# One x transpose moved to ScalarE's DMA queue, and weight loads issued ahead of the x pieces, in the opening of a gated attention-mix kernel

## Chip, cores and metric

The kernel runs on one core of a Trainium2 chip. The metric is device time in microseconds (us). The first execution ever of the kernel before took 999.06 us. It is in the 475.19 us that was known when the prediction was made (without it, 475.07). "The profile" is one recorded execution; its span is about 1.7 us shorter than the device time of the same execution. A *landing* is the moment at which the last of a load's 16 DMA engines has reported its part, as the recorded semaphore updates of the trace have it.

## The reference

Two attention blocks share the input x (2048 x 1024, bf16) and are mixed by a gate computed from x:

```python
g = sigmoid((x * gate_w).sum(-1, keepdims=True))
a = linear_attention(x, A_wqkv, A_wo)          # phi(q), phi(k), 32 heads of 32
b = dilated_sliding_attention(x, B_wqkv, B_wo) # 8 keys, 2 apart
return g * a + (1 - g) * b
```

Only the first product matters here: block A's keys, x @ wqkv[:, 1024:2048], which is the first real work of the kernel.

## The kernel before

The matmuls of this kernel take x with the contraction dimension on the partitions, so x is transposed while it is loaded (`dma_start_transpose`). For the first four row tiles (512 rows) the load is cut along the contraction into four *quarters* k. Each quarter has one x piece (512 rows x 256 columns, 256 KB) and two weight loads (half 0 and half 1 of the key columns, 256 KB each). Quarter 0's x piece comes in two transposes of 256 rows.

```python
load_wk(nc.scalar, 0, 0)                 # quarter 0, half 0: ScalarE's queue
with tc.manual_schedule(engines={SP}):   # everything else: SyncE's queue, in this order
    load_xT(0, 0, 2)                     # quarter 0, rows 0..255
    load_xT(0, 2, 4)                     # quarter 0, rows 256..511
    load_wk(nc.sync, 0, 1)
    for k in range(1, 4):
        load_xT(k, 0, 4)
        load_wk(nc.sync, k, 0)
        load_wk(nc.sync, k, 1)
    for t in range(4, NB):               # the other row tiles, whole rows
        nc.sync.dma_start_transpose(out=xT[:, :, t * P:(t + 1) * P], in_=rows(x, t * P, (t + 1) * P))
    # ... cut: further loads ...
```

TensorE first runs 34 junk matmuls on a tile of ones. Then it takes the quarters in turn, 16 matmuls each, and after them the other row tiles:

```python
warm_up(34)
first = [bank_k(i) for i in range(8)]
for k in range(4):
    for half in range(2):
        for t in range(4):
            for kt in (2 * k, 2 * k + 1):
                project(first[4 * half + t], t, kt, half)
            # ... cut: at k == 3, phi of the finished bank ...
```

A quarter can start when its x piece and its half-0 weights have landed.

## Time and profile before

| | before |
|---|---|
| median, the 3 runs known when the prediction was made (999.06 is one of them) | 475.19 us |
| TensorE busy, of a span of 473.4 us | 466.0 us |
| TensorE starts real matmuls | 4.74 us |
| quarter 1 starts | 10.33 us |

The page of the kernel before, its busy times and its chain of work that ended last:

```profile
PE 466.0 (98%) x5731; PEld 244.6 (52%) x5762; DVE 277.7 (59%) x602; ACT 169.0 (36%) x272; POOL 15.3 (3%) x30
...
PE 97%; DMA 1%; SPq 1%; issue 0%; ACT 0%
```

TensorE is on the chain nearly throughout, so a change to the loads can matter only where TensorE waits for one. The timeline of TensorE, first 24 us of the kernel before (start, duration, engine, line, operation, count, and in brackets the idle time ahead of it with what ended it):

```profile
1.11 3.81 PE L174 MATMUL warm<-onesb 128*128 128x128 bf16 x34 [1.11 <-DVE onesb L165]
4.74 4.11 PE L168 MATMUL pk_ps<-WkA,xT 128*128 128x512 bf16 x15
10.33 13.97 PE L168 MATMUL pk_ps<-WkA,xT 128*128 128x512 bf16 x63 [1.48 <-DMA WkA<-in_A_wqkv_dram]
```

(One of quarter 0's 16 matmul records is missing.) The only idle stretch of these 24 us after the start is the 1.48 us ahead of quarter 1, ended by a WkA load. The chain of the first 40 us says where that load came from (start, duration, what; a DMA line runs from the issue to the landing):

```profile
0.80 1.30 SPq L94
...
2.15 1.25 SPq L94
...
3.44 0.58 SPq L98
...
4.07 1.24 SPq L94
...
5.36 4.93 DMA WkA<-in_A_wqkv_dram
...
10.33 10.73 PE pk_ps L168 x49
```

SPq is SyncE's queue at work issuing: L94 is a transpose, L98 a weight load. The weights of quarter 1 had to wait behind three transposes of about 1.25 us each and a weight load. Issued at 5.36, they landed at 10.29.

### The profile page before, as it was taken

How to read it: one execution, taken by the hardware profiler on the slowest of the kernel's cores; microseconds unless marked ns; L12 is line 12 of the kernel's file. 1: busy time of each engine (PE TensorE's matmuls, PEld its weight loads, DVE VectorE, ACT ScalarE, POOL GpSimd, SP SyncE). 2: the span in 40 equal slices, each digit the busy share in tenths (PEclk: the TensorE clock that was granted, in tenths of full speed). 3: DMA queues.
4: the chain of work that ended last, by engine and by line, in shares of the span. 5: the costliest groups of instructions: out<-in, count | busy, mean ns of one | idle time of the engine just before them, and what ended most of it. 6: DMA issues, size and time to landing. Idle time of an engine off the chain costs nothing.

```text
span 473.4 us, 13138 instructions
## 1 busy us (share of the span) xinstructions
PE 466.0 (98%) x5731; PEld 244.6 (52%) x5762; DVE 277.7 (59%) x602; ACT 169.0 (36%) x272; POOL 15.3 (3%) x30
## 2 busy tenths in 40 slices
PE   7999999999999999999999999999999999999997
PEld 5444444444444444445666666666664444444444
DVE  0496689991329999999567676767560049800000
ACT  1343321102443333333555555555551134221122
POOL 2300000500000000000000000000000000000000
PEclk9999999999999999999999999999999999999999
DMA  8999980000644233627327455442663923221111
GB/s 168 231 225 381 349 269 0 0 1 0 204 133 111 96 137 126 161 96 241 106 57 101 81 85 94 102 91 51 91 167 73 200 90 78 68 55 45 35 34 45
DMA packets 98780, 55.40 MB, mean 117 GB/s; under 512 B 70178, under 2 KB 90658, under 8 KB 98722
## 3 DMA queue, kind: packets, MB, share of 16 engines
q1 hardware_dynamic: 93554, 50.10, 42.3%
q10 hardware_dynamic: 5168, 4.46, 2.9%
q8 instruction: 45, 0.74, 0.7%
q14 instruction: 13, 0.11, 0.1%
HBM read 26.10 MB, written 15.86 MB: 89 GB/s over the span
## 4 chain that ended last, share of the span: by engine, by line
PE 97%; DMA 1%; SPq 1%; issue 0%; ACT 0%
PE q_ps L387 26%; PE d_ps L584 12%; PE p_ps L294 12%; PE g_ps L219 12%; PE e_ps L584 11%; PE pk_ps L168 11%; PE p_ps L330 9%; PE po L466 2%; PE s2b L444 2%; DMA WkA<-in_A_wqkv_dram 1%; SPq L94 1%; PE kv_ps L239 0%; PE w_ps L282 0%; SPq L98 0%; ACT osb L589 0%
## 5 line engine op out<-in xcount | busy, mean ns | idle before, releaser
L387 PE MATMUL q_ps<-xT,WqB 64*64 64x512 bf16 x1024 | 68.3, 377 | 0.0
L387 PE MATMUL q_ps<-xT,WkB 64*64 64x512 bf16 x1024 | 67.9, 377 | 0.0
L153 DVE TENSOR_SCALAR e<-e 128x512 f32<-128x512 f32 x64 | 27.1, 423 | 64.5 <-ACT e L152 64.5
L294 PE MATMUL p_ps<-WvB,xT 128*128 128x512 bf16 x250 | 57.3, 379 | 0.5 <-issue 0.3
L168 PE MATMUL pk_ps<-WkA,xT 128*128 128x512 bf16 x251 | 55.9, 383 | 1.7 <-DMA WkA<-in_A_wqkv_dram 1.5
L219 PE MATMUL g_ps<-pk,xrow 128*128 128x512 bf16 x251 | 55.2, 379 | 0.3
L449 ACT ACTIVATE PT<-s2b 128x928 bf16<-128x928 f32 (+4 forms) x40 | 34.1, 854 | 45.6 <-PE s2b L444 45.6
L451 DVE TENSOR_TENSOR PT<-PT,mask 128x928 bf16<-128x928 bf16 (+4 forms) x40 | 23.6, 590 | 37.8 <-ACT PT L449 37.8
L330 PE MATMUL p_ps<-WqA,xT 128*128 128x512 bf16 x187 | 43.1, 379 | 0.3
L168 PEld LDWEIGHTS <-xT 128*128 128x128 bf16 x256 | 25.1, 99 | 32.0 <-issue 2.5
L584 PEld LDWEIGHTS <-pqT 128*128 128x128 bf16 x272 | 26.0, 98 | 29.8 <-issue 0.4
L584 PEld LDWEIGHTS <-OBT 128*128 128x128 bf16 x272 | 26.0, 98 | 29.4
L219 PEld LDWEIGHTS <-xrow 128*128 128x128 bf16 x256 | 25.1, 98 | 30.2
L294 PEld LDWEIGHTS <-xT 128*128 128x128 bf16 x256 | 24.6, 98 | 30.0 <-issue 0.9
L387 PEld LDWEIGHTS <-WkB 64*64 64x64 bf16 x1024 | 31.8, 107 | 15.4 <-issue 0.4
L387 PEld LDWEIGHTS <-WqB 64*64 64x64 bf16 x1024 | 31.5, 106 | 15.5 <-issue 0.9
L152 ACT ACTIVATE e<-pk_ps 128x512 f32<-128x512 f32 x32 | 18.9, 597 | 42.0 <-PE pk_ps L168 36.6
L299 ACT CAST tmp<-p_ps 128x512 bf16<-128x512 f32 x32 | 18.7, 589 | 37.6 <-PE p_ps L294 31.2
L584 PE MATMUL d_ps<-WoA,pqT 128*128 128x512 bf16 (+1 forms) x133 | 30.7, 370 | 0.2
L584 PE MATMUL d_ps<-WoB,OBT 128*128 128x512 bf16 (+1 forms) x134 | 30.7, 370 | 0.1
L330 PEld LDWEIGHTS <-xT 128*128 128x128 bf16 x192 | 18.8, 98 | 22.7
L584 PE MATMUL e_ps<-WoB,OBT 128*128 128x512 bf16 (+2 forms) x133 | 29.7, 363 | 0.2
(62 smaller groups left out, 484.1 us busy)
## 6 DMA issues: line engine op xcount, KB each, us to landing
vd<-tmp SPq DMA_DIRECT2D x16, 264.0 KB
xrow<-in_A_x_dram SPq DMA_DIRECT2D x4, 1024.0 KB
out_dram<-osb ACTq DMA_DIRECT2D x31, 128.0 KB
pqd<-tmp SPq DMA_DIRECT2D x12, 256.0 KB
WvA<-in_A_wqkv_dram SPq DMA_DIRECT2D x2, 1024.0 KB
WoA<-in_A_wo_dram SPq DMA_DIRECT2D x2, 1024.0 KB
WvB<-in_B_wqkv_dram SPq DMA_DIRECT2D x2, 1024.0 KB
WqA<-in_A_wqkv_dram SPq DMA_DIRECT2D x2, 1024.0 KB
```

The costliest lines, as they stand in the source:

```text
L152: nc.scalar.activation(out=e[:], in_=pj[:], func=ACT.Exp)
L153: nc.vector.tensor_scalar(out=e[:], in0=e[:], scalar1=1.0, scalar2=1e-6, op0=ALU.min, op1=ALU.add)
L168: nc.tensor.matmul(pj[:], lhsT=xT[:, kt, t * P:(t + 1) * P], rhs=WkA[half][:, kt, :], start=(kt == 0), stop=(kt == KT - 1))
L219: nc.tensor.matmul(pj[:], lhsT=xrow[:, t, kt * P:(kt + 1) * P], rhs=pk[:, t, half * 512:(half + 1) * 512], start=(t == 0), stop=(t == NB - 1))
L294: nc.tensor.matmul(st["pj"][:], lhsT=xT[:, kt, t * P:(t + 1) * P], rhs=WvB[half][:, kt, :], start=(kt == 0), stop=(kt == KT - 1))
L299: nc.scalar.copy(out=v[:, half * 16:(half + 1) * 16, 0:Dh], in_=st["pj"][:].rearrange("p (h e) -> p h e", h=16))
L330: nc.tensor.matmul(st["pj"][:], lhsT=xT[:, kt, t * P:(t + 1) * P], rhs=WqA[half][:, kt, :], start=(kt == 0), stop=(kt == KT - 1))
L387: nc.tensor.matmul(banks[o][64 * j:64 * j + 64, :], lhsT=lhsT(r, kt, j), rhs=rhs(r, kt), start=first and kt == 0, stop=kt == KT - 1, skip_ ...
L444: nc.tensor.matmul(s2b[64 * par:64 * par + 64, pair, :, o:o + w], lhsT=kts[c][r, par, k0:k0 + 64], rhs=qz[r, :, par, q0 % 512:q0 % 512 + w ...
L449: nc.scalar.activation(out=pt[:, :, 0:W_], in_=s2b[:].rearrange("p a b s -> p (a b) s")[:, :, 0:W_], func=ACT.Exp, scale=SCALE)
L451: nc.vector.tensor_tensor(out=pt[:, :, 0:W_], in0=pt[:, :, 0:W_], in1=mask[:, None, base:base + W_].broadcast_to([P, 4, W_]), op=ALU.mult)
L584: nc.tensor.matmul(st["ps"][:, 0:n], lhsT=lhsT, rhs=W[c0 // 512][:, c, c0 % 512:c0 % 512 + n], start=(side == 0 and c == 0), stop=(side == ...
```

## The change

The intent is to get those weights issued sooner: one of the three transposes goes to ScalarE's queue, which issues nothing after its one weight load (0.82 to 1.27) in the opening, and each quarter's half-0 weights go ahead of its x piece.

```diff
-    def load_xT(k, t0, t1):
-        nc.sync.dma_start_transpose(out=xT[:, 2 * k:2 * k + 2, t0 * P:t1 * P],
-                                    in_=rows(x, t0 * P, t1 * P)[:, 2 * k * P:(2 * k + 2) * P])
+    def load_xT(eng, k, t0, t1):
+        eng.dma_start_transpose(out=xT[:, 2 * k:2 * k + 2, t0 * P:t1 * P],
+                                in_=rows(x, t0 * P, t1 * P)[:, 2 * k * P:(2 * k + 2) * P])
 ...
     load_wk(nc.scalar, 0, 0)
+    load_xT(nc.scalar, 0, 2, 4)
     with tc.manual_schedule(engines={SP}):
-        load_xT(0, 0, 2)
-        load_xT(0, 2, 4)
+        load_xT(nc.sync, 0, 0, 2)
         load_wk(nc.sync, 0, 1)
         for k in range(1, 4):
-            load_xT(k, 0, 4)
             load_wk(nc.sync, k, 0)
+            load_xT(nc.sync, k, 0, 4)
             load_wk(nc.sync, k, 1)
```

## The prediction

> **What bounds the kernel now.** TensorE: the page's busy table gives PE 466.0 of 473.4 us, and the chain that ended last is 97% PE. Outside the opening TensorE hardly idles (the waits view names one real wait: 1.5 us for a WkA load). So only the opening can move, and any change of the moment at which TensorE becomes continuously busy passes to the end one for one.
>
> The opening, from timeline, chain and landing records: junk matmuls run to 4.74 us; quarter 0 (16 matmuls) runs 4.74 to 8.85, the first four at a pitch of 0.43 us, the rest at 0.216; then idle until 10.33, because WkA quarter 1 half 0 (issued by SyncE at 5.36) landed at 10.29. From there TensorE is continuous. Landings: x piece 0 first half 4.70, second half 5.30; WkA quarter 0 3.73 and 6.98; x piece 1 7.99. A transpose costs its queue 1.24 to 1.30 us to issue, a weight load 0.5 to 0.6.
>
> **Intent.** Taking one transpose (1.25 us) from SyncE and issuing quarter 1's weights before its x piece puts that load at about 2.7 us instead of 5.36. At most it recovers the 1.48 us idle.
>
> **What the change adds.** The built program shows what the diff does not: transposes on two queues are chained. ScalarE's transpose waits for the completion of SyncE's first one, and SyncE's next transpose (x piece 1) waits for the completion of ScalarE's. The Trainium skill, page "DMA: Bandwidth & Descriptors", section "Silent corruption: two transposing streams in flight at once", says that the later stream's first transpose must wait for the earlier stream's full completion; the trace of before, with one stream, cannot show it. So three transposes that overlapped (issues 0.80, 2.15, 4.07) now run one after another, each with issue, transfer and completion exposed.
>
> Estimate from before's durations:
> - First half lands about 4.6 (before 4.70).
> - ScalarE issues then; issue to landing was 3.15 us for the 256-token piece (2.15 to 5.30): second half lands about 7.8 (before 5.30).
> - SyncE issues x piece 1 then; issue to landing was 3.9 us (4.07 to 7.99), perhaps a little less on a quiet queue: lands about 11.6 (before 7.99).
>
> TensorE: first four matmuls 4.74 to 6.45, idle to 7.8, twelve more (12 x 0.216) to 10.4, idle to about 11.7 to 12, then continuous. Quarter 1 starts about 1.3 to 1.8 us later than 10.33. If the first gap keeps the matmuls at 0.43 us, quarter 0 ends near 13 and the loss is 2.7 us. Later quarters: before, x and weights of a quarter arrived about every 2.5 us while TensorE takes 3.45 us, so no new stall after quarter 1 is expected; xrow and later loads shift but have slack.
>
> **Predicted time: 476.8 us (before 475.2), 80% range 475.4 to 478.8.** Chance of faster by over 2%: 0.005; within 2%: 0.985; slower by over 2%: 0.01.
>
> **What would show the steps.** Right: ScalarE's transpose issue appears at about 4.7, not 1.3; SyncE's queue is empty from about 3.3 to 7.8; a first TensorE gap before x's second half, a second one ended by x piece 1 (an xT transpose, no longer WkA); WkA quarter 1 half 0 lands before 7; from about 12 everything is before's timeline shifted by a constant. Wrong: transposes overlap, or quarter 1 starts before 10.3.
>
> **What would make it wrong.** Lone transposes land much faster than 3.15 and 3.9 us (then a tie or small gain); before's late WkA landing (engines spread from 8.60 to 10.29) is a stall that another order avoids or meets again at x piece 1; ScalarE issues transposes more slowly than SyncE; the gap delays the 0.216 us pace; a later quarter stalls because SyncE's queue restarts near 8 us.

## The result, and the profile after

The changed kernel's median is 475.87 us (475.70 to 476.76, 6 runs), the kernel before's 474.51 us in the five runs counted with it (474.73 if the 999.06 is counted too). The ratio is 1.003, 95% interval 1.0017 to 1.0044: slower, by an amount far inside 2%. A ratio here is the mean time of one kernel's fast runs over that of the other's of the same rounds, so it is not quite the ratio of the medians.

The page after, the same two lines:

```profile
PE 466.4 (98%) x5731; PEld 244.3 (52%) x5762; DVE 277.7 (59%) x602; ACT 169.1 (36%) x272; POOL 15.4 (3%) x30
...
PE 97%; DMA 2%; issue 0%; ACT 0%
```

The work is unchanged; the chain's DMA share has grown, and SyncE's issuing has left the chain. The timeline of TensorE after:

```profile
4.72 1.91 PE L168 MATMUL pk_ps<-WkA,xT 128*128 128x512 bf16 x4
7.82 2.55 PE L168 MATMUL pk_ps<-WkA,xT 128*128 128x512 bf16 x11 [1.19 <-DMA xT<-in_A_x_dram]
11.02 13.28 PE L168 MATMUL pk_ps<-WkA,xT 128*128 128x512 bf16 x59 [0.65 <-DMA xT<-in_A_x_dram]
```

Where there was one gap there are now two, and both end with an x transpose, not with weights. The chain after:

```profile
0.80 3.46 DMA xT<-in_A_x_dram
...
4.28 3.49 DMA xT<-in_A_x_dram
...
7.79 3.18 DMA xT<-in_A_x_dram
...
11.02 10.91 PE pk_ps L168 x49
```

Three transposes run strictly one after another: each is issued 0.02 us after the one before it has landed. The timelines of ScalarE's and then SyncE's queue after agree:

```profile
4.28 1.29 ACTq L94 DMA_TRANSPOSE xT<-in_A_x_dram  x1
```

```profile
0.80 1.29 SPq L94 DMA_TRANSPOSE xT<-in_A_x_dram  x1
2.15 1.07 SPq L98 DMA_DIRECT2D WkA<-in_A_wqkv_dram  x2
7.79 1.25 SPq L94 DMA_TRANSPOSE xT<-in_A_x_dram  x1
```

ScalarE has issued its weight load by 1.26, but issues its transpose only at 4.28. SyncE stands still from 3.22 to 7.79. The weights that were late before are early now: in the landing records, quarter 1's half 0 lands at 6.71. But quarter 1 starts 0.69 us later than before (11.02 against 10.33), because its x piece now lands at 10.97 instead of 7.99. By the first matmul of the next stage the shift is 0.85 us (62.98 against 62.13), and at the end of the span it is 0.84 (474.2 against 473.4). From that matmul to the end both profiles take 411.2 us: everything after the opening is only carried along.

Call the wait of a transpose on one queue for the landing of a transpose on the other a *handover*. The changed kernel has two of them in the opening, ScalarE's behind SyncE's first and SyncE's next behind ScalarE's.

### The profile page after: what moved, and what is told of

Its sections match the earlier page's. It is cut to its first block, busy times and chain, and to the rows that moved or that the text cites. A ratio compares the mean times of both kernels' runs of the same rounds, so it can differ in the third digit from the quotient of the medians.

```text
span 474.2 us, 13138 instructions
## 1 busy us (share of the span) xinstructions
PE 466.4 (98%) x5731; PEld 244.3 (52%) x5762; DVE 277.7 (59%) x602; ACT 169.1 (36%) x272; POOL 15.4 (3%) x30
## 4 chain that ended last, share of the span: by engine, by line
PE 97%; DMA 2%; issue 0%; ACT 0%
PE q_ps L387 26%; PE d_ps L584 12%; PE p_ps L294 12%; PE g_ps L219 12%; PE e_ps L584 11%; PE pk_ps L168 11%; PE p_ps L330 9%; DMA xT<-in_A_x_dram 2%; PE po L466 2%; PE s2b L444 2%; PE kv_ps L239 0%; PE w_ps L282 0%; ACT osb L589 0%
```

## The experiments

The theory: the handovers cost the time; the new order of the loads, alone, costs nothing and gains a little. Rivals: the order itself delays x; ScalarE's queue is slow at transposes; two queues in use hinder each other at the DMA engines; the clock of TensorE. All kernels gave correct results. Each was timed in 5 rounds beside the kernel before, on the same chip for e1 to e4; e5 to e8; the three repeats; e9.

| run | handovers before quarter 1 | quarter 1 starts, us | median, us | before, us | ratio (95% interval) |
|---|---|---|---|---|---|
| changed kernel | 2 | 11.02 | 475.87 | 474.51 | 1.0030 (1.0017 to 1.0044) |
| e1_reorder | 0 | 9.09 | 473.91 | 474.51 | 0.9987 (0.9975 to 0.9999) |
| e2_move | 2 | 11.65 | 476.49 | 474.51 | 1.0050 (1.0036 to 1.0063) |
| e3_weights_act | 0 | 9.61 | 474.22 | 474.51 | 0.9994 (0.9982 to 1.0006) |
| e4_x_act | 0 | 12.26 | 477.21 | 474.51 | 1.0061 (1.0049 to 1.0073) |
| e5_mirror | 0 | 9.51 | 474.24 | 474.94 | 0.9989 (0.9976 to 1.0001) |
| e6_one_handover | 1 | 9.77 | 474.69 | 474.94 | 0.9996 (0.9983 to 1.0009) |
| e7_four_handovers | 4 | 16.54 | 481.42 | 474.94 | 1.0134 (1.0117 to 1.0151) |
| e8_four_sync | 0 | 10.43 | 475.20 | 474.94 | 1.0012 (0.9999 to 1.0024) |
| before_again | 0 | 9.46 | 474.30 | 474.79 | 0.9995 (0.9983 to 1.0008) |
| after_again | 2 | 12.03 | 476.71 | 474.79 | 1.0037 (1.0025 to 1.0050) |
| e1_again | 0 | 9.23 | 473.99 | 474.79 | 0.9987 (0.9973 to 1.0001) |
| e9_filled_gap | 2 | 10.55 | 476.46 | 474.87 | 1.0033 (1.0018 to 1.0049) |

### The two halves of the change, each alone: e1 and e2

e1_reorder takes the order of the change without the move:

```diff
     load_wk(nc.scalar, 0, 0)
-    load_xT(nc.scalar, 0, 2, 4)
     with tc.manual_schedule(engines={SP}):
         load_xT(nc.sync, 0, 0, 2)
+        load_xT(nc.sync, 0, 2, 4)
```

> The second half of the change alone: each quarter's first weights ahead of its x piece, all transposes on SyncE, so no transpose waits for another queue. Theory (handovers between queues cost the time, the order does not): x piece 1 is issued at about 4.6 us and lands at 8.3 to 8.9, WkA quarter 1 half 0 before it; TensorE's quarter 1 starts at 8.9 to 9.3 instead of 10.33 (before) and 11.02 (after); time about 1.0 to 1.5 us below before. Rival (weights ahead of x delay the x pieces): quarter 1 starts at 10.3 or later, waits for xT, time at or above before.

Measured: 473.91 us, 0.6 below before (1.0 to 1.5 had been expected; a likely reason is before's own late load, below: in its repeat quarter 1 starts at 9.46, only 0.37 after e1's 9.09). The timeline of TensorE shows no gap left, one unbroken group from the end of the warm-up to past quarter 3:

```profile
4.83 19.53 PE L168 MATMUL pk_ps<-WkA,xT 128*128 128x512 bf16 x84
```

So the order does not delay x enough to matter: x piece 1 lands at 8.97, and quarter 0 lasts until then.

e2_move takes the move without the order:

```diff
         for k in range(1, 4):
-            load_wk(nc.sync, k, 0)
             load_xT(nc.sync, k, 0, 4)
+            load_wk(nc.sync, k, 0)
             load_wk(nc.sync, k, 1)
```

> The first half of the change alone: the second transpose on ScalarE's queue, SyncE's order as before. Theory: ScalarE's transpose is issued when the first one has landed (about 4.3) and lands at 7.8, x piece 1 lands at about 11.0 as in the changed kernel, and WkA quarter 1, now issued behind it at about 9.1, lands at 11.5 to 12.2; quarter 1 starts then; time 0.5 to 1.2 us above the changed kernel, 1.6 to 2.3 above before. Rival (the new order of the loads is what cost the time): at or below before.

Measured: 476.49 us, 2.0 above before and 0.6 above the changed kernel. (One of its six runs, 478.34 with a granted clock of 0.996, lies 1.8 above the others.) The chain of e2_move:

```profile
0.80 3.29 DMA xT<-in_A_x_dram
...
4.12 2.73 DMA xT<-in_A_x_dram
...
6.87 1.25 SPq L94
...
8.16 3.45 DMA WkA<-in_A_wqkv_dram
```

The two handovers stand at the head of the chain, and the weights then wait behind the delayed transpose. The four versions fit a sum: order alone 0.9987, move alone 1.0050, both 1.0030 and (repeat) 1.0037. The product of the first two is 1.0037. The move costs about 2 us, the order gives back about 0.6. That 0.6 is a net gain. In the changed kernel, where quarter 1's weights are issued ahead, ScalarE's transpose took 3.49 us from issue to landing; in e2, with one weight load fewer issued before it, 2.73.

### Relieving SyncE with ordinary loads: e3

Against e1; quarters 2 and 3 keep the order of the kernel before:

```diff
     load_wk(nc.scalar, 0, 0)
+    load_wk(nc.scalar, 0, 1)
+    load_wk(nc.scalar, 1, 0)
     with tc.manual_schedule(engines={SP}):
         load_xT(nc.sync, 0, 0, 2)
         load_xT(nc.sync, 0, 2, 4)
-        load_wk(nc.sync, 0, 1)
 ...   (cut: the rest of the loop)
```

> SyncE relieved by moving ordinary loads instead: quarter 0's second and quarter 1's first weight load on ScalarE's queue, all transposes on SyncE, no handover. Theory: transposes are issued at 0.8, 2.1 and 3.4, x piece 1 lands at 7.5 to 8.5, both weight loads before it; quarter 1 starts at about 8.9, time 1.2 to 1.5 us below before. Rival (two queues in use at once slow each other at the DMA engines): x's halves land later than 4.70 and 5.30 by a microsecond or more and the gain is under 0.5 us.

Measured: 474.22 us, 0.3 below before and inside the noise. Here the rival's numbers came true. The halves of x landed at 5.78 and 6.97 instead of 4.70 and 5.30, and TensorE's first matmul waited until 5.82. The transposes were issued on time (0.80, 2.16, 3.44), so the delay is in the transfer. The Trainium skill, page "DMA: Bandwidth & Descriptors", section "Issuing engines are not separate DMA queues", says that DMAs from all issuing engines run on the same 16 DMA engines and that a second issuer saves only sequencer time. This run agrees: two more weight loads issued early on the other queue (three in all) cost the first transposes 1.1 and 1.7 us.

### Is ScalarE's queue bad at transposes? e4 and e5

e4_x_act puts all five transposes of the x pieces on ScalarE and the other weights on SyncE (against the changed kernel):

```diff
     load_wk(nc.scalar, 0, 0)
+    load_xT(nc.scalar, 0, 0, 2)
     load_xT(nc.scalar, 0, 2, 4)
+    for k in range(1, 4):
+        load_xT(nc.scalar, k, 0, 4)
     with tc.manual_schedule(engines={SP}):
-        load_xT(nc.sync, 0, 0, 2)
         load_wk(nc.sync, 0, 1)
         for k in range(1, 4):
             load_wk(nc.sync, k, 0)
-            load_xT(nc.sync, k, 0, 4)
             load_wk(nc.sync, k, 1)
```

> All five transposes of the four x pieces on ScalarE's queue, all weights but the first on SyncE; only one handover, at SyncE's transpose of row tile 4, needed by TensorE only near 19 us. Theory: ScalarE issues them without waits at 1.25 us each from 1.3; x lands at about 4.7, 5.9 and 8.5; quarter 1 starts at about 8.9 to 9.3, no gap later; time 0.8 to 1.5 us below before. Rival (ScalarE's queue is slow at transposes, or issues them late): x's second half lands at 7 or later again, time at or above the changed kernel.

Measured: 477.21 us, the opposite of what the theory had said. The chain of e4_x_act:

```profile
1.34 6.06 DMA xT<-in_A_x_dram
...
7.45 4.75 PE pk_ps L169 x15
```

The first transpose was issued at 1.34 without any handover, but took until 7.40 to land. By 2.82 SyncE had issued four weight loads and ScalarE one, 1.25 MB, which share the DMA engines with it. Its last two transposes took 2.67 and 3.08 us to issue. The late landing is not the whole loss: TensorE's first seven matmuls then came about 0.43 us apart, and quarter 1 began at 12.26 although its x piece had landed at 11.02. This run cannot tell crowding from a slow ScalarE queue, so e5 was built: the opening of e1 with the two queues exchanged, same order, no crowd ahead of the transposes.

```diff
-    load_wk(nc.scalar, 0, 0)
-    with tc.manual_schedule(engines={SP}):
-        load_xT(nc.sync, 0, 0, 2)
+    load_wk(nc.sync, 0, 0)
+    with tc.manual_schedule(engines={mybir.EngineType.Activation}):
+        load_xT(nc.scalar, 0, 0, 2)
 ...   (all of e1's opening on nc.scalar; an issue-order edge keeps row tile 4 behind it)
```

> The opening of e1_reorder with the two queues exchanged: ScalarE issues all five transposes and seven weight loads in the same order, SyncE the first weight load and then the row tiles. One handover, at row tile 4, which TensorE needs only near 19.8 us. This takes the crowding of e4_x_act away. Theory (ScalarE's queue is as good for transposes as SyncE's): halves of x land at 4.7 to 5.3 and 5.3 to 6.0, quarter 1 starts at 9.0 to 9.8, time within 0.7 us of e1_reorder (473.2 to 474.6). Rival (transposes from ScalarE are slow in themselves): the issues take over 2 us each or the halves land past 6.5, and the time is at or above the changed kernel, 475.9.

Measured: 474.24 us, ratio 0.9989 against e1's 0.9987. ScalarE's first two transposes took 1.28 and 1.29 us to issue and landed at 4.43 and 5.60. ScalarE's queue is as good for transposes as SyncE's. That leaves the crowd as the likely cause of e4's late landing, which no run isolated further. The one handover that e5 has, at row tile 4, cost TensorE nothing: SyncE issued that tile at 15.14, it landed at 18.98, and TensorE reached it at 19.88. (What TensorE did wait for in e5, 1.02 us, was quarter 0's half-1 weights, which landed at 7.66.)

### The number of handovers: e6, e7 and e8

e6_one_handover has both halves of piece 0 on ScalarE, followed there by the next two weight loads, and x piece 1 as SyncE's first transpose. (An issue-order edge between the transposes keeps the scheduler from exchanging them; it is not a wait.)

```diff
     load_wk(nc.scalar, 0, 0)
+    load_xT(nc.scalar, 0, 0, 2)
     load_xT(nc.scalar, 0, 2, 4)
+    load_wk(nc.scalar, 0, 1)
+    load_wk(nc.scalar, 1, 0)
     with tc.manual_schedule(engines={SP}):
-        load_xT(nc.sync, 0, 0, 2)
-        load_wk(nc.sync, 0, 1)
-        load_wk(nc.sync, 1, 0)
         load_xT(nc.sync, 1, 0, 4)
```

> The changed kernel with one handover instead of two: both halves of x piece 0 on ScalarE, followed there by the next two weight loads; x piece 1 is SyncE's first transpose and waits for the second half. Theory (each handover exposes one whole transpose, about 2.7 to 3.5 us): halves land at 4.7 to 5.3 and 5.7 to 6.3, x piece 1 is issued at once then and lands 3.2 us later at 9.0 to 9.6, quarter 1 starts there; time 1.0 to 1.8 us below the changed kernel (474.1 to 474.9), about level with before. Rival (it is ScalarE's use that costs, not the number of handovers): at 475.5 or above.

Measured: 474.69 us, 1.2 below the changed kernel and level with before. The chain of e6:

```profile
2.63 3.09 DMA xT<-in_A_x_dram
...
5.80 3.92 DMA xT<-in_A_x_dram
...
9.77 20.30 PE pk_ps L178 x93
```

One handover is left (SyncE issues at 5.80, when ScalarE's second has landed at 5.72). x piece 1 took 3.92 us here, with two weight loads underway beside it, so it landed at 9.72, 0.1 us later than expected.

e7_four_handovers splits piece 0 into four transposes of 128 rows on alternating queues; e8_four_sync is its control, all on SyncE:

```diff
         load_xT(nc.sync, 0, 0, 1)
         load_wk(nc.sync, 0, 1)
         load_wk(nc.sync, 1, 0)
-        load_xT(nc.sync, 0, 1, 2)      # e8
+        load_xT(nc.scalar, 0, 1, 2)    # e7
         load_xT(nc.sync, 0, 2, 3)
-        load_xT(nc.sync, 0, 3, 4)      # e8
+        load_xT(nc.scalar, 0, 3, 4)    # e7
         load_xT(nc.sync, 1, 0, 4)
```

> Four handovers: x piece 0 in four transposes of 128 rows, alternating SyncE, ScalarE, SyncE, ScalarE, then x piece 1 on SyncE. Theory: first lands at 3.6 to 4.1, then 2.3 to 2.9 us for each further one (9.2 or so for the third, 11 to 12.5 for the fourth), x piece 1 another 3.2 later; quarter 1 starts at 14.3 to 15.8; time 3.3 to 4.8 us above the changed kernel (479 to 481). Rival (the order of the loads or DMA bandwidth sets the opening): under 477.

> Control for e7_four_handovers: the same four small transposes and the same order of loads, all on SyncE, no handover. Theory: nothing of e7's loss is due to smaller transposes; the fourth lands at 6.5 to 7.3, x piece 1 at 9 to 9.8, quarter 1 starts at 9.0 to 9.9; time 473.8 to 474.8, 4.5 to 6.5 us below e7. Rival (small transposes are slow): over 476.

Measured: e7 481.42 us, e8 475.20 us, 6.2 us apart. The timeline of TensorE in e7:

```profile
4.58 0.59 PE L179 MATMUL pk_ps<-WkA,xT 128*128 128x512 bf16 x2
7.29 0.60 PE L179 MATMUL pk_ps<-WkA,xT 128*128 128x512 bf16 x2 [2.12 <-DMA xT<-in_A_x_dram]
9.89 1.03 PE L179 MATMUL pk_ps<-WkA,xT 128*128 128x512 bf16 x2 [2.00 <-DMA xT<-in_A_x_dram]
12.30 12.07 PE L179 MATMUL pk_ps<-WkA,xT 128*128 128x512 bf16 x42 [1.37 <-DMA xT<-in_A_x_dram]
```

Every handover shows as a gap. From issue to landing they took 3.35, 2.58, 2.38 and 2.97 us. Both kernels missed their expectations slightly, and both misses teach something.

e7 lost more than the handovers: x piece 1 had landed at 15.24, but quarter 1 started at 16.54, because the last ten matmuls of quarter 0 ran at a pitch of 0.43 us. The stretches of e7 (bounds, length, busy time of PE and the other engines, granted clock PEclk, DMA share, GB/s) show the clock:

```profile
8.00:12.00 4.00, 1.03 (x2) 0.13 (x2) 0.00 (x0) 0.00 (x0) 2.00 (x5) 0.50 0.15 33
12.00:18.00 6.00, 5.70 (x14) 2.11 (x15) 0.00 (x0) 0.00 (x0) 4.82 (x16) 0.50 0.74 161
```

e8 was 0.4 us above its range. Its profile points to the issuing: a transpose cost its queue about the same to issue whatever its size. The timeline of SyncE in e8 shows four of them issued in a row:

```profile
3.25 5.11 SPq L96 DMA_TRANSPOSE xT<-in_A_x_dram  x4
```

That group is the last three transposes of 128 rows and then x piece 1 (1.19, 1.25, 1.25 and 1.30 us, the last with four times the rows). So the fourth small transpose was issued only at 5.77 and landed at 8.21 (expected 6.5 to 7.3); the ten matmuls that were left of quarter 0 ran on from there to 10.43, where quarter 1 starts. x piece 1, issued at 7.06 instead of e1's 4.58, landed at 10.14, just before.

### Repeats, and the clock: before_again, after_again, e1_again, e9

The three kernels were run again, unchanged, together on one chip.

> The kernel before, unchanged, as a copy: the noise floor of the comparison, and a second profile. The ratio to before should hold 1.000 within 0.0015. Open: whether the late landing of WkA quarter 1 half 0 at 10.29 us (some DMA engines at 8.6, the last at 10.29) is usual. If it is a property of this order of loads, quarter 1 starts at 10.0 to 10.6 again; if it was a chance stall, quarter 1 starts at 8.9 to 9.6 and the profiled span is about a microsecond shorter.

> The changed kernel, unchanged, as a copy, on the same chip as e1_again: a second profile of the two handovers. ScalarE's transpose lands at 7.4 to 8.0 and x piece 1 at 10.7 to 11.3 again; time 0.8 to 1.5 us above before and 1.4 to 2.4 us above e1_again.

> e1_reorder again, on the same chip as the two kernels it is compared with: 0.3 to 1.2 us below before, no gap in TensorE's opening after 4.9 us, quarter 1 starting at 8.9 to 9.5. If its gain over before was chance, the ratio to before holds 1.000 within its interval and lies above 0.9995.

before_again gave 0.9995: the floor of the comparison. Its profile, however, differs from before's. Quarter 1's weights landed at 9.42 there and not at 10.29, and quarter 1 started at 9.46:

```profile
9.46 14.84 PE L168 MATMUL pk_ps<-WkA,xT 128*128 128x512 bf16 x67 [1.06 <-DMA WkA<-in_A_wqkv_dram]
```

In both records some of the DMA engines finish that load over a microsecond ahead of the last (8.60 to 10.29 in before, 8.27 to 9.42 in before_again). Similar stragglers appear at other loads in other runs, such as quarter 0's half 1 in e1_again (6.08 to 7.37), where TensorE waited 0.49 us for it though no gap had been expected. What makes them straggle was not found. So the idle that the change could have recovered is 1.0 to 1.5 us, not a fixed 1.48.

e1_again gave 0.9987, as e1 did. This version is the fastest in both series, though by only 0.13% against before. The interval excludes 1 in one of the two series and just includes it in the other; the profiles, in which quarter 1 starts 9.09 and 9.23 against 10.33 and 9.46, say why.

after_again gave 476.71 us, again slower than both, by 1.9 and 2.7 us: more than the 0.8 to 1.5 and 1.4 to 2.4 expected. The handovers are those of the first profile (issues at 0.80, 4.32 and 7.80, landings at 7.79 and 11.23). But in the profiled execution the clock also fell. The stretches of after_again:

```profile
5.00:8.00 3.00, 0.71 (x4) 0.18 (x3) 0.00 (x0) 0.00 (x0) 0.00 (x0) 0.95 0.59 159
8.00:12.00 4.00, 3.98 (x11) 1.45 (x11) 0.00 (x0) 0.00 (x0) 2.25 (x6) 0.61 0.65 131
```

and its timeline of TensorE:

```profile
4.52 1.03 PE L168 MATMUL pk_ps<-WkA,xT 128*128 128x512 bf16 x4
7.83 16.45 PE L168 MATMUL pk_ps<-WkA,xT 128*128 128x512 bf16 x66 [2.29 <-DMA xT<-in_A_x_dram]
```

Here TensorE was at full pace from 4.52, so its first four matmuls were done early and the gap was 2.29 us instead of 1.19. After it, eight matmuls came at 0.43 us apart, quarter 0 ended at 12.0, and x piece 1, landed at 11.23, had to wait 0.8 us for it. Quarter 1 started at 12.03 instead of 11.02. The Trainium skill, page "TensorE: Matmul & The Clock Gate", section "What's actually happening", says that TensorE's clock gate watches a free-running window of activity, so that the moment of the switch differs from run to run. The profiles agree in the effect: the first real matmuls had a pitch of 0.43 us in the first profiles of before and after, 0.22 in both kernels' repeats.

Does that clock explain the upper ones of the changed kernel's runs (476.7 to 476.9, four of five with a granted clock of 0.996, against 475.6 to 476.0 at 1.0)? In the profiled execution the clock was 0.50 from 7.7 to 11.1; by an estimate from that, half clock for 3.4 of 475 us makes a mean of 0.996, so one such stretch would account for the clock of these runs. e7's runs point the same way, the lower clock with the longer time: two at 0.989 took 482.01 and 482.41, two at 0.993 took 480.67 and 480.82. e9 fills the first gap with junk matmuls:

```diff
                     for t in range(4):
+                        if k == 0 and half == 0 and t == 2:
+                            for i in range(24):
+                                nc.tensor.matmul(first[4][:, 0:P], lhsT=onesb[:], rhs=onesb[:], start=True, stop=True)
                         for kt in (2 * k, 2 * k + 1):
```

> The changed kernel with 24 junk 128-column matmuls on TensorE between row tiles 1 and 2 of quarter 0 (into a bank whose first real matmul clears it), so that TensorE is hardly idle while ScalarE's transpose lands; the queues and both handovers are as in the changed kernel. Theory (the changed kernel's upper runs, 476.7 to 476.9 with a granted clock of 0.996, are those in which the 2.3 us gap drops TensorE's clock): no run shows 0.996, all lie at 475.4 to 476.2, quarter 0's later matmuls follow at 0.216 us, and quarter 1 still starts at 10.8 to 11.4 because x piece 1 lands no earlier. Rival (the upper runs come from the DMA side, a later landing of x piece 1): runs still spread to 476.7 and above.

Measured: 476.46 us (476.09 to 476.80). The granted clock was 0.999 or more in all six runs, quarter 0's later matmuls followed at 0.216 us, and quarter 1 started at 10.55 (expected 10.8 to 11.4), so filling the gap kept the clock. The time did not come down, though: five of the six runs lie above the expected 475.4 to 476.2. The timeline of TensorE in e9 shows a wait that no other profile had there:

```profile
16.47 7.71 PE L168 MATMUL pk_ps<-WkA,xT 128*128 128x512 bf16 x34 [0.33 <-DMA WkA<-in_A_wqkv_dram]
```

Quarter 2's half-1 weights, issued at 11.03, landed at 16.43, and TensorE was ready for them at about 15.99 (15.77 for the start of the matmul before, plus 0.216). Quarter 2 itself had started 0.2 us late, at 14.24, when its x piece landed at 14.20. Even so, by the first matmul of the next stage e9 is only 0.10 us behind the changed kernel's first profile (63.09 against 62.98). The other half microsecond of its longer span (474.9 against 474.2) lies outside the opening: the waits of e9 have 0.5 us at `po` (L469), in block B, that no other profile has. From the first matmul of the next stage to the end, twelve of the fourteen profiles take 411.2 to 411.3 us, e9's 411.8 and e5's 412.0; e5's profiled run, 475.05, was also about 0.8 above its other four. What makes this late difference was not looked into.

So the low clock is shown as a cost of the gap in the profiles of after_again and e7, but it is not the only cause of the changed kernel's upper runs: one run of after_again at clock 1.0 took 476.71 too. How much belongs to the clock, to stragglers and to the late difference stays open.

What was not tried: transposes on two queues without the wait. The price of the wait is therefore read from the number of handovers, not from taking it away.

## Why the prediction was right or wrong

- **The bound and the place: right.** Only the opening moved. The shift at the next stage (0.85 us) equals that of the span (0.84 us).
- **The hidden waits: right.** The built program chains the transposes, and the chain after shows them issued 0.02 us after the one before has landed. The Trainium skill, page "DMA: Bandwidth & Descriptors", section "Silent corruption: two transposing streams in flight at once", gives the reason for the wait.
- **The landings: near, one of them by luck.** First half 4.26 (predicted 4.6), second half 7.77 (7.8), x piece 1 at 10.97 (11.6). The second half is right because two errors cancel: it was issued 0.3 us earlier than predicted and took 3.49 us instead of 3.15. The mis-sized term of the rest is x piece 1's time from issue to landing, put at 3.9 us "perhaps a little less on a quiet queue". It measured 3.18 after, 3.43 in after_again and 2.94 in e2, where the loads issued before it had all landed, and 3.92 in e6 with weight loads in flight. The 3.9 of before was taken while two earlier loads were still landing (at 5.30 and 6.98).
- **The size: the total inside its range, the start of quarter 1 not in the first profile.** Quarter 1 was predicted 1.3 to 1.8 us later; it was 0.69 later in the first profile, and 1.70 against before's first (2.57 against before_again) in the repeat. The predicted 1.6 us compares with 1.4 us between the medians of the first comparison and 1.9 in the repeat. The repeat's 476.71 next to the predicted 476.8 is luck: in its profile quarter 1 was late because quarter 0 ran slowly, not because x piece 1 landed late.
- **The side remark on the clock: right that it could happen.** It was predicted that quarter 0 might end near 13 at a loss of 2.7 us. In after_again it ended at 12.0, since eight and not twelve matmuls were slow. The way there was another one, though: the clock was full before the gap and fell in it, where the prediction had it not yet risen.
- **"No new stall after quarter 1": not always.** The first profile after has a pause of 0.12 us within quarter 1, and e9 had one at quarter 2's half-1 weights.
- **"At most it recovers the 1.48 us idle": too high as a typical figure.** The repeat of before idled 1.06 us there.

## What to carry to other kernels

Before moving a DMA transpose to a second queue, look in the built program for what it will wait on: in every program here transposes on two queues ran one after another, and each handover exposes an issue, a transfer and a completion, here 2.4 to 3.9 us. Keep all transposes that are needed soon on one queue, whichever it is, and get the weights through by order, as e1 does. Ordinary loads can go to the second queue, but issued too early they delay the transposes (by 1.1 and 1.7 us in e3).

## What the Trainium skill lacked or had wrong

- Page "DMA: Bandwidth & Descriptors", section "Silent corruption: two transposing streams in flight at once": it says to wait but not what the wait costs. Here each transpose issued after a handover took 2.38 to 3.92 us from issue to landing, and none of it overlapped the transpose before it.
- The same page, section "Issuing engines are not separate DMA queues", calls the issue time that a second queue saves usually small relative to the DMA. For the opening's transposes it was not: most took 1.2 to 1.3 us to issue, almost regardless of size (128 x 256: 1.19; 512 x 256: 1.25), while those after a handover landed 2.4 to 3.9 us after their issue began.
- Page "TensorE: Matmul & The Clock Gate", section "Why this matters for your kernels", warns of idle gaps over about 3 us. Here shorter gaps were followed by a lower clock: 2.29 us in after_again (granted clock 0.50 from 7.7 to 11.1) and 2.12 us in e7 (0.52 in the same stretch). The length alone does not decide: in e2 a gap of 2.12 us (9.54 to 11.65) and in e8 one of 1.85 us left the clock at 1.00.
- No page that was read explains the straggling DMA engines for loads issued by SyncE or ScalarE: one 256 KB weight load whose engines finish between 8.60 and 10.29 us.
